# Attention chunks, weight conversion and the offset between two MLP token blocks: moving the second block from seven steps behind the first to four

## Chip, cores and metric

One core of a Trainium2 chip runs the whole kernel. The metric is the device time of one execution in microseconds; the three runs of the kernel before gave 1007.63, 1008.31 and 1009.01, median 1008.31.

## The reference

```python
state = alpha[:, :, t, :, None] * state + np.einsum('bhd,bhe->bhde', k[:, :, t], v[:, :, t])
y[:, :, t] = np.einsum('bhd,bhde->bhe', q[:, :, t], state)
...
h = x @ w_in                       # (3072, 384) @ (384, 2048)
g = h * (1.0 / (1.0 + np.exp(-h)))
x2 = g @ w_out
...
gate = 1.0 / (1.0 + np.exp(-(x2 @ w_gate)))
out = (gate * (x2 @ w_val)) @ w_out2   # d_ff 1536
```

A gated linear attention (4 sequences, 8 heads, 768 tokens, head size 48) feeds an MLP with silu and then a gated MLP, for 3072 tokens of 384 features. Everything is float32 to the user, and the weights arrive as 64-bit floats.

## The kernel before

**Attention.** The tokens are cut into 24 chunks of 128, six to a sequence. For a chunk c, `load_chunk` and `load_values` (L215, L226) fetch its data through SP's queue. `prep` (L262) makes the decays: step 0 is a reversed scan on VectorE (L277), two tiny instructions (L279, L280) and a multiply of k (L285); step 1 a second scan (L287); step 2 a multiply of q (L290). Up to chunk 8 (`ALONE`) the multiplies are GpSimd's, from chunk 9 on VectorE's. `scores` (L297) issues TensorE's transposes of k and the products of k and q; with `apart` the transposes go to a buffer of pool `ps_h`, otherwise to the bank that also takes results. `scores_done` (L318) multiplies by the causal mask on VectorE (L323), copies the transposes on ScalarE (L326) and checks the decays there (L260). `results` (L330) issues the products that give the chunk's output and its addition to the state; `state` (L357) adds that on VectorE (L363, L365) and decays the state (L367, GpSimd up to chunk 8). `y_out` (L377) copies the output on ScalarE and rearranges it with six DMAs (L385, L387). `x_out` (L389) splits it into a rounded part (ScalarE, L394) and a remainder (L396, GpSimd up to chunk 8, then VectorE). The scores of chunk c+1 use the PSUM banks that hold chunk c's addition to the state.

**MLP.** Every product of float32 data is three TensorE products of rounded parts and remainders (`mm3`, L546, L549 to L551). Tokens go in six blocks of 512, so a block is four chunks. One step of the main loop (L754) takes a block b and a slice f of 128 hidden features: `mm_in` (L559) is nine products into h; `act` (L565) is silu (L568), a rounded copy `gh` (L576, ScalarE) and the remainder `gl` (L577, VectorE); `mm_out` (L582) is nine products with `w_out`, issued two steps later through the list `pend`. The list `items` (L725) gives the order: LAG = 7 steps of block 0 alone, then blocks 0 and 1 in turn, then the last LAG slices of block 1, then the other blocks. At a block's end `x2_out` (L595) copies the output from PSUM.

**Weights.** Each slice's 64-bit weights are converted on the way to a slot of rounded part and remainder (class `Way`, L409). The list at L641 has one slot in each of groups 0 to 2 (`in` 0, `in` 1, `out` 0) and two in groups 3 to 16 (`in` g-1 and `out` g-2), one in group 17. A group is made in six bits (`bit`, L507) or two halves (`half`, L526). The first half of group j holds the first two VectorE instructions of group j+1 and one of group j (L459, L494, L461); the second half holds the last two of group j (L496, L497) and the third of group j+1 (L463); ScalarE has L451, L482 and the rounded copy L486, GpSimd the remainder L504. The scratch tiles of a group are reused two groups later.

**Order.** It is written out by hand. In the prefix (L683 to L703), iteration c issues the scores of chunk c+1, the decays of c+2, `x_out` of c-1, the results of c, and then CONV[c] bits. Then each step issues `mm_in`, the chunk work put at (step, place), `act`, `mm_out`, more chunk work, and in the first LAG steps one more half; `act` itself has a half ahead of `gl` (L572) and closes it behind (L578). The tables SCORES and RESULTS (L47, L48) say at which (block, slice, place) a chunk's work stands; `steps` (L706) derives decays and `x_out` from them. Every engine works through its own instructions in the order in which they are issued.

Of the kernel before, what the change touches and what calls it, by code (L numbers as in the profile page):

```python
# [22 lines left out]
NC = NT // C  # L23
# [6 lines left out]
NF1 = FF1 // P  # L30
# [4 lines left out]
NB = len(BLOCKS)  # L35

LEAD = 5
LAG = 7

ALONE = 8  # L40
WARM = 3

BITS = 6
SINGLE = 3
CONV = {1: 5, 2: 5, 3: 6, 4: 5}

SCORES = {6: (0, 1, 0), 7: (0, 3, 0), 8: (0, 5, 0), 9: (1, 10, 0), 10: (1, 11, 1), 11: (1, 13, 0)}  # L47
RESULTS = {5: (0, 0, 0), 6: (0, 2, 0), 7: (0, 4, 0), 8: (0, 6, 0), 9: (1, 11, 0), 10: (1, 12, 1), 11: (1, 14, 0)}  # L48
for _c in range(12, NC):
    SCORES[_c] = (_c // 4 - 1, (0, 4, 8, 11)[_c % 4], 0)  # L50
    RESULTS[_c] = (_c // 4 - 1, (2, 6, 10, 13)[_c % 4], 0)

# [125 lines left out]
def gated_attention_then_mlps(ctx: ExitStack, tc: tile.TileContext, qka, a0, v, w_in, w_out, w_gate, w_val, w_out2, out):  # L178
# [17 lines left out]
    def X(i, dtype=F32):  # L196

        return xp.tile([P, NK, N], dtype, tag=f"x{i}", name=f"x{i}", bufs=1)
# [27 lines left out]
    def load_values(c):  # L226
        vt[c] = ap.tile([P, H, D], F32, tag="v", name="v", bufs=4)
        nc.sync.dma_start(out=vt[c], in_=v[c].rearrange("t (h e) -> t h e", e=D))
# [19 lines left out]
    def warm(n):  # L248

        w = bank(1)[:P]  # L250
        for i in range(n):
            nc.tensor.matmul(w, dg[:, :P], dg[:, :N], start=True, stop=True)
# [41 lines left out]
    def last_of(c):  # L294
        return c % CB == CB - 1
# [343 lines left out]
    with tc.manual_schedule():  # L639
        way1 = Way(  # L640
            [[("in", 0)], [("in", 1)], [("out", 0)]] + [[key for key in (("in", j), ("out", j - 1)) if key[1] < NF1] for j in range(2, NF1 + 1)],  # L641
            lambda j: X(2 * j % 4, U32).rearrange("p k t -> p (k t)"),
            lambda j: X(2 * j % 4 + 1, U32).rearrange("p k t -> p (k t)"),
            lambda n: wp.tile([P, 2, NK, P], F32R, tag="w", name="w"),
        )
        slots2 = [(name, f) for f in range(NF2) for name in ("gate", "val", "out2")]
        NX = 4
        way2 = Way(
            [slots2[n : n + 2] for n in range(0, len(slots2), 2)],
            lambda j: bp["b"].tile([P, 4 * SW], U32, tag="raw", name="raw2", bufs=3),  # L650
            lambda j: bp["b"].tile([P, 4 * SW], U32, tag="tmp", name="tmp2", bufs=3),
            lambda n: (wp if n >= NX else bp["x"]).tile([P, 2, NK, P], F32R, tag="w" if n >= NX else "wx", name="w2"),
        )

        load_chunk(0)
        load_values(0)
        nc.sync.dma_start(out=a0s, in_=a0)
        constants()
        warm(WARM)
        for c in range(1, 4):  # L660
            load_chunk(c)
            load_values(c)
            if c > 1:
                way1.load(c - 2)

        late = []

        def states():
            while late and (last_of(late[0]) or late[0] + 1 in AE):
                c = late.pop(0)  # L670
                if not last_of(c):
                    state(c)

        def results_done(c):
            late.append(c)
            if c >= LEAD:
                states()
            y_out(c)
            if c + 4 < NC:
                load_chunk(c + 4)  # L680
                load_values(c + 4)

        for p0, p1 in ((0, 2), (2, NP)):  # L683
            for s in range(3):
                prep(0, s, p0, p1, nc.vector)
            scores(0, 0, True, p0, p1)
        for s in range(3):
            prep(1, s)
        scores_done(0)
        for c in range(LEAD):  # L690
            scores(c + 1, (c + 1) % 2, True)
            states()
            prep(c + 2, 0)
            scores_done(c + 1)
            prep(c + 2, 1)
            prep(c + 2, 2)
            if c:
                x_out(c - 1)
            results(c, c % 2)
            results_done(c)  # L700
            for _ in range(CONV.get(c, 0)):
                way1.bit()
        states()  # L703
        way1.n_half = 2 * SINGLE

        def steps(items):  # L706

            at = {x: i for i, x in enumerate(items)}
            todo = {}

            def put(i, place, what, c):
                todo.setdefault((i, place), []).append((what, c))

            for c, (b, f, end) in SCORES.items():
                put(at[b, f], end, "scores", c)
                if c > LEAD + 1:
                    put(at[b, f] - 3 if c != ALONE + 1 else at[0, LAG - 2], 2, "prep0", c)
                    put(at[b, f] - 2, 2, "prep1", c)
            for c, (b, f, end) in RESULTS.items():
                put(at[b, f], end, "results", c)  # L720
                put(at[b, f] + 1 if c != ALONE else at[1, NF1 - LAG - 1], 1, "x_out", c)
            put(0, 1, "x_out", LEAD - 1)
            return todo

        items = [(0, f) for f in range(LAG)]  # L725
        for f in range(LAG, NF1):
            items += [(0, f), (1, f - LAG)]
        items += [(1, f) for f in range(NF1 - LAG, NF1)] + [(b, f) for b in range(2, NB) for f in range(NF1)]
        todo = steps(items)

        def tensor(i, place):
            for what, c in todo.get((i, place), ()):
                g = int(c <= ALONE)
                if what == "scores":
                    scores(c, g, False)
                elif what == "results":
                    results(c, g)

        def others(i, place):
            for what, c in todo.get((i, place), ()):  # L740
                if what == "scores":
                    scores_done(c)
                elif what == "results":
                    results_done(c)
                elif what == "x_out":
                    x_out(c)
                elif what == "prep0":
                    prep(c, 0)
                    states()
                elif what == "prep1":  # L750
                    prep(c, 1)
                    prep(c, 2)

        for i, (b, f) in enumerate(items):  # L754
            if (b, f) == (NB - 1, 0):
                at_stack.close()
                bp["b"] = main.enter_context(tc.tile_pool(name="bp", bufs=3))
                bp["x"] = main.enter_context(tc.tile_pool(name="bx", bufs=NX))
                way2.load(0)
                way2.n_half = -2  # L760
            h = mm_in(ps_h, "h", "in", b, f)
            tensor(i, 0)
            way = way1 if i < 2 * NF1 - LAG else way2 if b == NB - 1 else None
            act(b, f, h, None, "out", way)
            others(i, 0)
            others(i, 2)
            if len(pend) > 2:
                mm_out()
            tensor(i, 1)
            others(i, 1)  # L770
            if i < LAG:
                way1.half(True)
                way1.half(False)
            if (b, f) == (NB - 1, NF1 - 4):
                x2_split(0)
            if (b, f) == (NB - 1, NF1 - 1):
                x2_split(1)
        ps_v = None
        items = [(b, f) for f in range(NF2) for b in (0, 1)] + [(b, f) for b in range(2, NB) for f in range(NF2)]
        for b, f in items:  # L780
            if (b, f) == (1, NF2 - 1):
                x2_split(2)
            gate = mm_in(ps_h, "h", "gate", b, f)
            if b == 3 and f % 3 == 0 and f < 9:
                verdict(ps_n, f // 3)
            val = mm_in(ps_v or ps_h, "v" if ps_v else "h", "val", b, f)
            act(b, f, gate, val, "out2", way2 if b < 2 else None)
            if len(pend) > 2:
                mm_out()
            if (b, f) == (2, 1):  # L790
                ps_stack.close()
                ps_v = main.enter_context(tc.tile_pool(name="ps_v", bufs=2, space=PSUM))
                ps_n = main.enter_context(tc.tile_pool(name="ps_n", bufs=1, space=PSUM))
            if f == NF2 - 4 and 1 < b < NB - 1:
                x2_split(b + 1)
        while pend:
            mm_out()
# [46 lines left out]
```

## Time and profile before

| | us |
|---|---|
| median of three runs (lowest, highest) | 1008.31 (1007.63, 1009.01) |
| the profiled execution | 1007.8 |
| its span, first to last instruction | 1006.1 |
| TensorE (PE) busy | 957.5 |
| VectorE (DVE) busy | 521.8 |
| ScalarE (ACT) busy | 385.7 |
| GpSimd (POOL) busy | 127.1 |
| mean granted TensorE clock | 0.975 |

In the rows below, times count from the span's start. A line of a timeline has start, length, engine, line of the kernel, operation, tile written and tiles read, their shapes and the number of instructions merged into it; in brackets is the idle time ahead of it and what ended that. A row of windows has the stretch and its length, then the busy time (with a count) of PE, PEld (weight loads), DVE, ACT and POOL, then the granted clock, the DMA engines' busy share and GB/s. SPq is the queue that issues DMAs.

### The profile page before, as it was taken

The page shows a single profiled execution, that of the slowest core. Times are in us where ns is not written, and L with a number is a line of the kernel's source. Part 1 is how long each engine was busy: PE and PEld are TensorE (multiplying, and loading weights), DVE is VectorE, ACT ScalarE, POOL GpSimd, SP SyncE. Part 2 cuts the span into 40 slices and gives each one's busy share as a digit, 9 for nine tenths or more (in the row PEclk, how much of TensorE's full clock was granted, in tenths as well). Part 3 has the DMA queues.
Part 4 walks back from the last instruction along what each step waited for, and adds up shares of the span by engine and source line. Part 5 has one row for each costly group of instructions (what it writes and reads, how often), then busy time and mean ns, then how long its engine had stood idle before and what let it go on. Part 6 is the DMA issues. An engine that isn't in the chain of part 4 may idle for free.

```text
span 1006.1 us, 12880 instructions
## 1 busy us (share of the span) xinstructions
PE 957.5 (95%) x5008; PEld 786.3 (78%) x5008; DVE 521.8 (52%) x782; ACT 385.7 (38%) x713; POOL 127.1 (13%) x117
## 2 busy tenths in 40 slices
PE   6577899999999999999999999999999999999996
PEld 4465678877888888888888888888888888888885
DVE  8999888464554454453589755663222222222221
ACT  3344566444433433443457443343222222221221
POOL 4554433200000000000033122220000000000000
PEclk8778899999999999999999999999999999999999
DMA  7665352012112112000322111100100000000001
GB/s 184 174 164 160 107 165 83 0 45 87 44 51 80 44 44 78 18 8 13 130 95 94 63 64 64 63 0 1 63 1 1 32 1 0 32 1 1 32 1 35
DMA packets 40038, 58.38 MB, mean 58 GB/s; under 512 B 5216, under 2 KB 28928, under 8 KB 39968
## 3 DMA queue, kind: packets, MB, share of 16 engines
q1 hardware_dynamic: 39968, 57.47, 19.4%
q8 instruction: 41, 0.67, 0.3%
q14 instruction: 29, 0.24, 0.1%
HBM read 48.02 MB, written 4.72 MB: 52 GB/s over the span
## 4 chain that ended last, share of the span: by engine, by line
PE 85%; DVE 9%; issue 2%; POOL 1%; ACT 1%; DMA 1%; SPq 0%; DVEq 0%; POOLq 0%; ACTq 0%
PE h L549 12%; PE h L551 12%; PE h L550 12%; PE s L549 8%; PE s L551 7%; PE s L550 7%; PE y L551 4%; PE y L549 4%; PE y L550 4%; PE v L549 3%; PE v L551 3%; PE v L550 3%; PE s L310 2%; PE y L345 2%; PE y L338 2%
## 5 line engine op out<-in xcount | busy, mean ns | idle before, releaser
L549 PE MATMUL h<-x,w 128*128 128x512 f32 x582 | 228.5, 393 | 4.1 <-ACT w L486 2.3
L551 PE MATMUL h<-x,w 128*128 128x512 f32 x582 | 227.7, 391 | 1.5 <-POOL w L504 1.5
L577 DVE TENSOR_TENSOR gl<-g,gh 128x512 fp32r<-128x512 f32 x168 | 130.0, 774 | 190.8 <-ACT gh L576 190.8
L550 PE MATMUL h<-x,w 128*128 128x512 f32 x582 | 227.5, 391 | 0.0
L576 ACT ACTIVATE gh<-g 128x512 fp32r<-128x512 f32 x168 | 106.2, 632 | 157.9 <-DVE g L571 154.9
L549 PE MATMUL s<-gl,w 128*128 128x512 f32 x336 | 135.8, 404 | 1.5 <-DVE gl L577 1.5
L549 PEld LDWEIGHTS h<-x,w 128*128 128x128 f32 x582 | 109.8, 189 | 29.6 <-ACT w L486 3.5
L550 PE MATMUL s<-gh,w 128*128 128x512 f32 x336 | 132.0, 393 | 0.0
L551 PE MATMUL s<-gh,w 128*128 128x512 f32 x336 | 132.0, 393 | 0.0
L551 PEld LDWEIGHTS h<-x,w 128*128 128x128 f32 x582 | 109.6, 188 | 26.0 <-POOL w L504 2.8
L568 ACT ACTIVATE g<-h 128x512 f32<-128x512 f32 x96 | 57.2, 596 | 184.2 <-PE h L551 184.2
L550 PEld LDWEIGHTS h<-x,w 128*128 128x128 f32 x582 | 109.6, 188 | 23.0
L571 DVE TENSOR_TENSOR g<-v,g 128x512 f32<-128x512 f32 x46 | 31.8, 692 | 178.7 <-PE v L551 178.7
L504 POOL TENSOR_TENSOR w<-tmp,w 128x384 fp32r<-128x384 f32 x36 | 44.3, 1251 | 443.7 <-ACT w L486 443.7
L570 ACT ACTIVATE g<-h 128x512 f32<-128x512 f32 x72 | 43.1, 599 | 144.4 <-PE h L551 144.4
L549 PEld LDWEIGHTS s<-gl,w 128*128 128x128 f32 x336 | 63.5, 189 | 17.5 <-DVE gl L577 1.9
L551 PEld LDWEIGHTS s<-gh,w 128*128 128x128 f32 x336 | 63.7, 189 | 13.8
L550 PEld LDWEIGHTS s<-gh,w 128*128 128x128 f32 x336 | 63.7, 190 | 12.3
L550 PE MATMUL y<-gh,w 128*128 128x512 f32 x168 | 66.0, 393 | 0.0
L549 PE MATMUL y<-gl,w 128*128 128x512 f32 x168 | 65.9, 393 | 0.0
L551 PE MATMUL y<-gh,w 128*128 128x512 f32 x168 | 65.8, 391 | 0.0
L551 PE MATMUL v<-x,w 128*128 128x512 f32 x138 | 53.8, 390 | 0.0
(114 smaller groups left out, 1170.9 us busy)
## 6 DMA issues: line engine op xcount, KB each, us to landing
x<-in_moe_w_out SPq DMA_DIRECT2D x16, 384.0 KB, 4.4
x<-in_qka SPq DMA_DIRECT2D x12, 448.0 KB, 4.3
qk<-in_qka SPq DMA_DIRECT2D x11, 448.0 KB, 4.3
v<-in_v SPq DMA_DIRECT2D x24, 192.0 KB, 4.2
x<-in_moe_w_in SPq DMA_DIRECT2D x16, 288.0 KB, 3.7
raw<-in_moe_w_gate SPq DMA_DIRECT2D x12, 384.0 KB, 3.6
raw<-in_moe_w_val SPq DMA_DIRECT2D x12, 384.0 KB, 3.9
raw<-in_moe_w_out SPq DMA_DIRECT2D x12, 384.0 KB, 3.8
```

The costliest lines, as they stand in the source:

```text
L310: nc.tensor.matmul(S[c][:, j, p * C : (p + 1) * C], t[r : r + D, NP * C + p * C : NP * C + (p + 1) * C], t[r : r + D, p * C : (p + 1) * C] ...
L338: nc.tensor.matmul(y[:DP, p * C : (p + 1) * C], W[:, p], qk[c][:, p * C : (p + 1) * C], start=p == 0, stop=False, skip_group_check=True)
L345: nc.tensor.matmul(y[r : r + D, p * C : (p + 1) * C], vt[c][:, 2 * p + j], m[:, j, p % 2], start=first and p == 0, stop=True, skip_group_c ...
L504: nc.gpsimd.tensor_tensor(l, b[:, i * SW : (i + 1) * SW].bitcast(F32), h.bitcast(F32), op=ALU.subtract)
L549: nc.tensor.matmul(ps, wh, x_l, start=first, stop=False)
L550: nc.tensor.matmul(ps, wh, x_h, start=False, stop=False)
L551: nc.tensor.matmul(ps, wl, x_h, start=False, stop=last)
L568: nc.scalar.activation(g, h, AF.Silu)
L570: nc.scalar.activation(g, h, AF.Sigmoid)
L571: nc.vector.tensor_tensor(g, val, g, op=ALU.mult)
L576: nc.scalar.activation(gh, g, AF.Copy)
L577: nc.vector.tensor_tensor(gl, g, gh.bitcast(F32), op=ALU.subtract)
```

## The change

The second block starts four steps behind the first in place of seven. Chunks 5 to 8 are worked on one to a step in steps 0 to 3 (before: one in two steps, up to step 6). In the prefix 15 bits are converted in place of 21, three in every iteration; step 0 makes six bits in two lots, steps 1 to 3 a first half behind the chunk's state and decays and a second half at the step's end, both behind `gl` rather than around it. From step 4 on `act` takes one half for each step, and steps 6 and 7 get a second one. At the end of block 1, chunks 9 to 12 take one step each in its last four (before: chunks 9 to 11, and chunk 12 in block 2). Slices 14 and 15 of block 0 are issued one after the other. In blocks 0 and 1 the transposes go to `ps_h`. Tables X_OUT and DECAYS place what `steps` had derived.

```diff
-LAG = 7
+LAG = 4
...
-CONV = {1: 5, 2: 5, 3: 6, 4: 5}
-
-SCORES = {6: (0, 1, 0), 7: (0, 3, 0), 8: (0, 5, 0), 9: (1, 10, 0), 10: (1, 11, 1), 11: (1, 13, 0)}
-RESULTS = {5: (0, 0, 0), 6: (0, 2, 0), 7: (0, 4, 0), 8: (0, 6, 0), 9: (1, 11, 0), 10: (1, 12, 1), 11: (1, 14, 0)}
-for _c in range(12, NC):
+CONV = {0: 3, 1: 3, 2: 3, 3: 3, 4: 3}
+
+SCORES = {6: (0, 0, 1), 7: (0, 1, 1), 8: (0, 2, 1), 9: (1, 12, 0), 10: (1, 13, 1), 11: (1, 14, 1), 12: (1, 15, 1)}
+RESULTS = {5: (0, 0, 0), 6: (0, 1, 0), 7: (0, 2, 0), 8: (0, 3, 0), 9: (1, 13, 0), 10: (1, 14, 0), 11: (1, 15, 0), 12: (1, 15, 3)}
+
+X_OUT = {8: (1, 11), 11: (1, 15), 12: (2, 0)}
+
+DECAYS = {7: ((0, 0), (0, 0)), 8: ((0, 1), (0, 1)), 9: ((0, 2), (1, 10)), 10: ((1, 10), (1, 11)), 11: ((1, 12), (1, 13)), 12: ((1, 13), (1, 14))}
+for _c in range(13, NC):
...
-                    put(at[b, f] - 3 if c != ALONE + 1 else at[0, LAG - 2], 2, "prep0", c)
-                    put(at[b, f] - 2, 2, "prep1", c)
+                    first, then = (at[x] for x in DECAYS[c]) if c in DECAYS else (at[b, f] - 3, at[b, f] - 2)
+                    put(first, 2, "prep0", c)
+                    put(then, 2, "prep1", c)
...
-                put(at[b, f] + 1 if c != ALONE else at[1, NF1 - LAG - 1], 1, "x_out", c)
+                put(at[X_OUT[c]] if c in X_OUT else at[b, f] + 1, 1, "x_out", c)
...
-        for f in range(LAG, NF1):
+        for f in range(LAG, NF1 - 2):
             items += [(0, f), (1, f - LAG)]
+        items += [(0, NF1 - 2), (0, NF1 - 1), (1, NF1 - LAG - 2), (1, NF1 - LAG - 1)]
...
-                    scores(c, g, False)
+                    scores(c, g, items[i][0] < 2)
...
+        def convert(i):
+            if i == 0:
+                for _ in range(BITS // 2):
+                    way1.bit()
+            else:
+                way1.half(True)
+                way1.half(False)
...
-            way = way1 if i < 2 * NF1 - LAG else way2 if b == NB - 1 else None
+            way = way1 if LAG <= i < 2 * NF1 - LAG else way2 if b == NB - 1 else None
             act(b, f, h, None, "out", way)
             others(i, 0)
             others(i, 2)
+            if i < LAG:
+                convert(i)
             if len(pend) > 2:
                 mm_out()
-            tensor(i, 1)
-            others(i, 1)
-            if i < LAG:
-                way1.half(True)
-                way1.half(False)
+            for place in (1, 3):
+                tensor(i, place)
+                others(i, place)
+            if i < LAG or LAG + 2 <= i < LAG + 4:
+                convert(i)
```

## Rows read from the trace of the kernel before

**Rows 1.** Page: the span.
```profile
span 1006.1 us, 12880 instructions
```

**Rows 2.** Windows: prefix, steps 0 to 6, after (stretch, length, busy by engine, clock).
```profile
20.40:59.19 38.79, 23.93 (x232) 21.39 (x232) 36.72 (x52) 15.55 (x41) 22.33 (x22) 0.74 0.60 163
...
59.19:122.86 63.67, 50.09 (x305) 38.16 (x305) 57.27 (x73) 31.34 (x63) 28.04 (x24) 0.84 0.52 143
...
122.86:250.00 127.14, 122.60 (x656) 100.37 (x657) 81.80 (x124) 65.54 (x122) 25.43 (x21) 1.00 0.26 75
```

**Rows 3.** Waits of PE from 122.86 to 250 us: total, times, longest.
```profile
PE s L310 <- ACT x L600: 2.0, 1, 2.0
...
PE s L549 <- DVE gl L577: 1.5, 1, 1.5
```

**Rows 4.** Timeline, PE: step 8's first product and the tenth.
```profile
127.80 0.39 PE L549 MATMUL h<-x,w 128*128 128x512 f32 x1
...
129.84 0.39 PE L549 MATMUL s<-gl,w 128*128 128x512 f32 x1
```

**Rows 5.** Windows: a pair's halves; state; mask and first scan; second scan.
```profile
140.25:142.06 1.81, 1.81 (x9) 1.50 (x9) 1.81 (x3) 1.78 (x3) 0.00 (x0) 1.00 0.53 151
...
142.67:145.00 2.33, 2.33 (x12) 1.94 (x11) 2.29 (x5) 0.76 (x2) 0.15 (x1) 1.00 0.55 169
...
225.81:226.57 0.76, 0.76 (x4) 0.62 (x5) 0.71 (x3) 0.24 (x1) 0.00 (x0) 1.00 0.00 0
...
230.09:232.85 2.76, 2.76 (x14) 2.28 (x13) 2.69 (x6) 1.09 (x4) 0.00 (x0) 1.00 0.62 189
...
235.37:236.59 1.22, 1.22 (x6) 0.98 (x7) 1.22 (x2) 0.59 (x1) 0.00 (x0) 1.00 0.00 0
```

**Rows 6.** DVE by line, steps 0 to 6: busy, mean ns, idle before, releaser.
```profile
L463 DVE SCALAR_TENSOR_TENSOR x<-x 128x768 f32<-128x768 f32 x7 | 12.9, 1847 | 0.1
...
L459 DVE TENSOR_SCALAR x<-x 128x768 uint32<-128x768 uint32 x7 | 5.7, 808 | 5.6 <-POOL w L504 5.6
```

**Rows 7.** Timeline, DVE and POOL, end of step 1's conversion.
```profile
81.38 3.68 DVE L463 SCALAR_TENSOR_TENSOR x<-x 128x768 f32<-128x768 f32 x1
...
82.27 1.97 POOL L504 TENSOR_TENSOR w<-x,w 128x384 fp32r<-128x384 f32 x2
```

**Rows 8.** Timeline, DVE: first and fourth of the bits that leave.
```profile
47.07 2.10 DVE L459 TENSOR_SCALAR x<-x 128x384 uint32<-128x384 uint32 x1
...
50.46 0.36 DVE L494 TENSOR_SCALAR x<-x 128x384 uint16<-128x384 uint16 x1
```

**Rows 9.** Timeline: rounded copy, product, silu, copy of g.
```profile
81.49 0.94 ACT L486 ACTIVATE w<-x 128x384 fp32r<-128x384 f32 x2 [4.31 <-DVE x L497]
...
82.06 0.50 PE L549 MATMUL h<-x,w 128*128 128x512 f32 x1 [0.82 <-ACT w L486]
...
82.33 0.58 ACT L568 ACTIVATE g<-h 128x512 f32<-128x512 f32 x1
...
82.94 0.63 ACT L576 ACTIVATE gh<-g 128x512 fp32r<-128x512 f32 x1
```

**Rows 10.** Timeline, PE: small products behind three different waits.
```profile
64.65 2.05 PE L338 MATMUL y<-qk,state 112*112 112x128 f32 x8 [3.12 <-POOL state L367]
...
97.04 1.13 PE L338 MATMUL y<-x,state 112*112 112x128 f32 x8
...
77.41 1.20 PE L345 MATMUL y<-m,v 128*48 128x128 f32 x16 [1.69 <-ACT x L394]
```

**Rows 11.** Timeline, SP: four of a chunk's six result copies.
```profile
127.79 2.49 SPq L387 DMA_DIRECT2D xf<-xs  x4
```

**Rows 12.** Timeline: chunk 11's result, its x_out, block 2's first product.
```profile
235.37 0.60 ACT L382 ACTIVATE xs<-y 112x512 f32<-112x512 f32 x1 [0.63 <-PE y L345]
...
240.94 0.53 ACT L394 ACTIVATE x<-xf 128x384 fp32r<-128x384 f32 x1
...
242.31 0.47 PE L549 MATMUL h<-x,w 128*128 128x512 f32 x1 [0.60 <-DVE x L396]
```

## The prediction, made before the changed kernel was run

> **What bounds the kernel now.** I read the page first for the span, then the busy time of the engines over three stretches, then who keeps TensorE waiting, then VectorE's instructions by line, and last the timeline around single waits. "Step i" is the i-th pass of the main loop, T0 to T7 the start on TensorE of the first product of that step (59.19 us for T0, 122.86 us for T7), and a "group" is one entry of the conversion list (groups 0 to 2 hold one weight slot, 3 to 17 hold two). The profiled execution took 1007.8 us with a span of 1006.1 [rows 1]; the median of the three runs is 0.5 us above it.
>
> From T7 to 250 us TensorE is busy 122.60 of 127.14 us [rows 2], and the longest of its few waits are one of 2.0 and one of 1.5 us [rows 3]. Nine large products take 2.04 us there [rows 4], so a step (nine in, nine out) is 4.1 us of pure TensorE time. Ahead of T7 it is VectorE that is full: 36.72 of 38.79 us in the later prefix, 57.27 of 63.67 us in steps 0 to 6, with TensorE at a mean granted clock of 0.74 and 0.84 [rows 2]. So the time is, in essence, the moment at which VectorE lets TensorE run freely, plus the TensorE work then left.
>
> VectorE's 63.67 us hold more than work. Undisturbed, a pair of slots costs it 1.81 us in its first half and 2.33 us in its second, 4.1 us together; a chunk costs 0.76 (state), 2.76 (mask, first scan and what hangs on it) and 1.22 us (second scan), 4.7 together [rows 5]. In steps 0 to 6 one of the pair's six instructions alone averages 1847 ns, and the first of a pair stands idle 5.6 us in all behind GpSimd's subtraction of an earlier pair [rows 6]. Why: an instruction of VectorE on SBUF that starts while GpSimd works doesn't advance until GpSimd is done. The 3.68 us of the one at 81.38 end at 85.06, a little after GpSimd's 1.97 us ending at 84.24; undisturbed it ends within the 2.33 us of its half [rows 5, 7].
>
> The Trainium skill ("SBUF — State Buffer", section "SBUF: two separate sides") states this as a rule: one shared pair of ports, held for the whole instruction, the loser fully blocked. By that rule, with all of GpSimd's time added to VectorE's, the sum below would stand some 13 us higher. The trace agrees for this instruction but not for the stretch: 28.04 us of GpSimd fit beside 57.27 of VectorE in 63.67 us [rows 2].
>
> **The parts of the change.**
>
> *Prefix.* Six bits of conversion leave it (21 to 15). Four of them stood ahead of T0: the first starts at 47.07 us, the fourth at 50.46 and takes 0.36, so 3.75 us pass [rows 8]. The new bits of iteration 0 fill VectorE time that is nearly all busy already [rows 2], so nothing more is won: T0 moves from 59.2 to about 55.6. Bounds: 0 (if GpSimd's x_out ends last anyway) to 5.
>
> *Work put off.* At T7 now, seven products in and five out are done. By the new order the like point, TensorE free, with chunks up to 8 done, is T4: four in and two out. Six times 2.04 us, **+12.2 us**, come afterwards [rows 4]. Against that VectorE has three pairs fewer to make by then.
>
> *Steps 0 to 3.* This is the large term. Before, step i makes the pair that step i+2 multiplies; VectorE works a step behind TensorE and hardly ever waits for it. After, step i makes what step i+1 multiplies (group 3 in step 1, and `in` slot 2 is wanted in step 2). Then the two wait in turn. The chain, from before's rows: with the second half's last add done, ScalarE's rounded copy starts at 81.49 and the first product at 82.06 [rows 9]; the products then wait about 1 us for GpSimd's remainder (1.97 us for two slots [rows 7]), so 3.1 us in place of 2.04 until h is whole; silu 0.58 and the copy 0.63 us [rows 9]; only then `gl`, which now stands first in VectorE's order, and the state update behind it, which wants the chunk's results from TensorE. All the rest of the step's VectorE work, the conversion included, is queued behind these.
> The price depends on TensorE's clock. Behind a wait of 3.12 us eight small products took 2.05 us; without one the same eight took 1.13 [rows 10]. These are the two levels, 1.2 and 2.4 GHz. In the new steps 2 and 3 TensorE stands idle 4 us and more ahead of each step, so I take the lower level: h 4.3 us, results 3.7 (2.05 for the first eight, the rest partly recovered).
> Laid out by hand: step 0: VectorE's work 9.8 us (a state, a gl of 0.7, two scans, the second half of group 2, a mask, the first half of group 3, what is left of group 2's first half), 1.8 waiting for the first h, 2.6 behind GpSimd: 14.2, to 69.8. Step 1: gl 0.7, chunk 4.7, pair to its add 3.3, GpSimd 3.5: 12.2, to 82.0. Step 2: 0.6 to the first product, h and results 8.0, then state 0.8, first scan with its multiplies on VectorE 2.4, half a pair 1.8, mask 1.2, the two adds 1.5, GpSimd 1.7: 17.9, to 99.9. Step 3, without a scan or mask: 0.6, 8.0, 0.8, 1.8, 1.5, GpSimd 2.0: 14.7, to 114.6. T4 is 0.6 behind, **115.2**.
> The unknown is GpSimd: I charged 9.8 us of its roughly 22 in these steps (28.04 less three pairs at 1.97 [rows 2, 7]). In steps 0 to 6 VectorE lost about a third of GpSimd's time (nearest row, 28.04 us [rows 2]); that would be 7.3. I take the middle, 8.5: T4 is 113.9. Bounds: 7 and 22 of GpSimd; clock high or low, some 4.4.
>
> *After T4.* The first products run at the lower level: +2.0. Steps 4 to 7 make three pairs in 16.4 us of TensorE; with about 6 us for each (4.1 and a third of the 5.6 behind GpSimd [rows 5, 6]) and four gl VectorE needs 21, but a step's second products come two steps later, so TensorE has that much to go on: of the waits, today's 1.5 us [rows 3] falls away and about 0.5 comes, -1.0.
>
> *Chunks 9 to 12.* They move to the last four steps of block 1; chunk 12, moved ahead of block 2, is the same TensorE work earlier, cost 0. VectorE needs about 7.5 us for each (4.7, a gl, and the multiplies that GpSimd does for earlier chunks), in steps of 4.1 plus 3.7 for the chunk's products: covered. SP issues for each chunk six result copies (four of them 2.49 us [rows 11]) and its loads, some 5 us, under the step, here and in steps 0 to 3. The seam costs: chunk 11's ScalarE copy began at 235.37 and its x_out at 240.94, 5.6 us later, and block 2 waited 0.60 [rows 12], with a whole step between. Now only one mm_out (2.04), scores and results of chunk 12 lie between, and x_out is queued on ScalarE behind that chunk's checks: TensorE waits about 0.7 for the mask and 1.6 for x_out, 1.7 more than today; the 2.0 us wait at block 0's end [rows 3] loses some 0.3. **+1.4**; bounds 0 and 4. Transposes into an `h` buffer free TensorE of waits where it isn't the bound: 0.
>
> *Sum.* T4 113.9 + 12.2 - 122.9 = +3.2; + 2.0 - 1.0 + 1.4 = **+5.6**: 1013.4 for the profiled execution's 1007.8, **1013.5** as a median between this and its 0.5 more.
>
> **Rivals.**
> *VectorE stays fed (faster).* If gl and the state of steps 2 and 3 find their inputs ready, these steps cost VectorE's own work: about 11 and 8 us in place of 17.9 and 14.7. That takes 13.6 off: T4 100, and 1000 in all. For it: now VectorE idles only 6.4 us in steps 0 to 6, 5.6 of them behind GpSimd [rows 2, 6], and that idling should vanish as the chunk's work stands between the pairs. It decides at gl of steps 2 and 3: below 2 us of idle there it wins; half of it is 1006. Chance 0.30.
> *The clock holds (same).* If TensorE stays at the upper level, h and results take 2.2 us less in each of two steps and the 2.0 after T4 goes: -6.4, about 1007 to 1009. For it: 16 products behind a wait of 1.69 us took 1.20, no longer than at the upper level [rows 10]. Against: the 3.12 us above. Chance 0.13.
> *Steps 4 to 10 starve (slower still).* If `in` slots 5 and 6 come late, VectorE's 21 us against 16.4 show up as TensorE waits: up to +4.4, 1017. Chance 0.15, inside the slower cases.
> *The seam alone.* T4 comes out even and only block 2's start is late: 1010. Chance 0.10, slower too.
>
> **How the numbers follow.** The forecast has 0.32; with its two neighbours slower has 0.57, the seam and the starved steps included. A measurement of this kernel tells about 0.2% (2 us) from no change. The range goes from most of the fed case (1001) to the starved one with a full charge for GpSimd (1019), and leaves out the fully fed case and full blocking. The slower cases' own range is 1010 to 1019.
>
> **What would show it.** Right: first product of step 0 near 55.6; VectorE idle 3 us or more ahead of gl in steps 2 and 3; TensorE idle over 4 us ahead of steps 3 and 4, with a clock of 0.5 behind; T4 after 110; no idle of VectorE behind GpSimd's subtraction at a pair's start; block 2's first product waiting about 2 us. Wrong: T4 below 108 (the break-even, 122.9 less 12.2 less the 2.4 that follow), or gl in steps 2 and 3 without a wait.

## The result and the profile after

The change made the kernel slower: 1016.54 us median of four runs (1015.94 to 1018.67) against 1008.64 of the kernel before on the same chip, a ratio of 1.0084 with a 95% interval of 1.0066 to 1.0101. The forecast was 1013.5 within 1001 to 1019. The profiled execution took 1015.96 us with a span of 1014.2, against 1007.8 and 1006.1 [rows 1]. The changed file has four more lines ahead of the functions, so L463 in it is L459 of before, L501 is L497, L553 is L549, L581 is L577.

The windows of the changed kernel, cut at its own T0 and T4, answer to [rows 2]:

```profile
20.40:56.23 35.83, 25.15 (x233) 22.14 (x232) 30.29 (x50) 14.19 (x38) 24.16 (x22) 0.67 0.54 150
56.23:113.54 57.31, 34.33 (x251) 26.92 (x251) 40.18 (x59) 24.00 (x51) 21.57 (x19) 0.75 0.47 129
113.54:250.00 136.46, 133.31 (x716) 108.60 (x716) 93.32 (x140) 73.46 (x134) 29.77 (x26) 0.98 0.29 84
```

In steps 0 to 3 VectorE is busy 40.18 of 57.31 us (70%), where it had 57.27 of 63.67 (90%). Nothing is full in this stretch any more: TensorE 60%, GpSimd 38%, at a mean granted TensorE clock of 0.75. What VectorE waited for is in its waits from 56.23 to 135 us (total, times, longest):

```profile
DVE gl L581 <- ACT gh L580: 13.9, 3, 5.6
DVE x L463 <- DMA x<-in_moe_w_out: 8.9, 2, 6.2
DVE state L367 <- PE s L359: 2.2, 2, 1.2
```

And TensorE, from 55 to 330 us, answering to [rows 3]:

```profile
PE h L553 <- ACT w L490: 17.9, 3, 8.5
...
PE s L553 <- ACT x L604: 2.9, 1, 2.9
...
PE s L314 <- ACT x L604: 1.4, 1, 1.4
PE h L553 <- DVE x L400: 1.4, 1, 1.4
...
PE y L349 <- issue: 0.8, 1, 0.8
```

The first rows of the two lists belong together: TensorE waited three times, 17.9 us, for ScalarE's rounded weights (L490), which wait for VectorE's last add; VectorE waited three times, 13.9 us, for `gl`'s input, which waits for TensorE. The timeline of steps 2 to 4 shows one turn after the other:

```profile
81.47 0.96 DVE L501 TENSOR_TENSOR x<-x 128x768 f32<-128x768 f32 x1
...
82.46 0.94 ACT L490 ACTIVATE w<-x 128x384 fp32r<-128x384 f32 x2 [3.52 <-DVE x L501]
83.03 0.80 PE L553 MATMUL h<-x,w 128*128 128x512 f32 x1 [8.46 <-ACT w L490]
...
87.60 0.60 ACT L572 ACTIVATE g<-h 128x512 f32<-128x512 f32 x1 [4.21 <-PE h L555]
...
88.89 0.69 DVE L581 TENSOR_TENSOR gl<-g,gh 128x512 fp32r<-128x512 f32 x1 [5.60 <-ACT gh L580]
...
99.49 0.80 PE L553 MATMUL h<-x,w 128*128 128x512 f32 x1 [5.28 <-ACT w L490]
...
105.35 0.69 DVE L581 TENSOR_TENSOR gl<-g,gh 128x512 fp32r<-128x512 f32 x1 [5.60 <-ACT gh L580]
...
113.54 0.80 PE L553 MATMUL h<-x,w 128*128 128x512 f32 x1 [4.13 <-ACT w L490]
...
120.03 0.56 DVE L463 TENSOR_SCALAR x<-x 128x768 uint32<-128x768 uint32 x1 [6.23 <-DMA x<-in_moe_w_out]
```

The first product of each of these steps takes 0.80 us in place of the 0.50 in [rows 9]: the lower clock (granted 0.50 over the nine products of steps 2 and 3 and the first twelve from step 4 on), after waits of 8.46, 5.28 and 4.13 us. From the first product of step 2 to silu 4.57 us pass. The last line is a wait that the prediction did not have.

The starts of steps, read from the first product of each in the timeline of TensorE, serve as milestones for all runs. By step 12 every version has done the same TensorE work (12 slices in, 10 out, chunks up to 8); by step 35, in block 2, the seam is behind it too.

| profiled execution | step 0 | 2 | 4 | 5 | 12 | 35 | span |
|---|---|---|---|---|---|---|---|
| before | 59.2 | 73.4 | 94.9 | 103.4 | 146.0 | 258.1 | 1006.1 |
| after | 56.2 | 83.0 | 113.5 | 120.7 | 150.4 | 266.5 | 1014.2 |

So of 8.1 us in the span, 4.4 are lost ahead of step 12 and 4.0 between step 12 and step 35; behind that the two run alike within 0.3 us.

### The profile page after: what moved, and what is told of

It reads as the page before. It is cut to its first block, busy times and chain, and to the rows that moved or that the text cites. A ratio compares the mean times of both kernels' runs of the same rounds, so it can differ in the third digit from the quotient of the medians.

```text
span 1014.2 us, 12894 instructions
## 1 busy us (share of the span) xinstructions
PE 959.3 (95%) x5008; PEld 788.2 (78%) x5008; DVE 510.4 (50%) x782; ACT 386.2 (38%) x713; POOL 126.2 (12%) x117
## 3 DMA queue, kind: packets, MB, share of 16 engines
q1 hardware_dynamic: 39968, 57.47, 19.3%
## 4 chain that ended last, share of the span: by engine, by line
PE 87%; DVE 4%; DMA 2%; POOL 2%; issue 1%; ACT 1%; SPq 1%; DVEq 0%; ACTq 0%; POOLq 0%
PE h L553 13%; PE h L555 13%; PE h L554 13%; PE s L553 8%; PE s L554 7%; PE s L555 7%; PE y L555 4%; PE y L554 4%; PE y L553 4%; PE v L553 3%; PE v L554 3%; PE v L555 3%; PE y L349 2%; PE y L342 2%; PE s L314 2%
## 5 line engine op out<-in xcount | busy, mean ns | idle before, releaser
L553 PE MATMUL h<-x,w 128*128 128x512 f32 x582 | 230.1, 395 | 20.4 <-ACT w L490 17.9
L581 DVE TENSOR_TENSOR gl<-g,gh 128x512 fp32r<-128x512 f32 x168 | 130.8, 779 | 197.2 <-ACT gh L580 197.2
L553 PEld LDWEIGHTS h<-x,w 128*128 128x128 f32 x582 | 110.4, 190 | 44.8 <-ACT w L490 18.9
L553 PE MATMUL s<-gl,w 128*128 128x512 f32 x336 | 134.7, 401 | 3.0 <-ACT x L604 2.9
L508 POOL TENSOR_TENSOR w<-tmp,w 128x384 fp32r<-128x384 f32 x36 | 44.3, 1251 | 431.9 <-ACT w L490 431.9
L553 PEld LDWEIGHTS s<-gl,w 128*128 128x128 f32 x336 | 63.3, 188 | 18.9 <-ACT x L604 3.3
L553 PE MATMUL y<-gl,w 128*128 128x512 f32 x168 | 65.5, 390 | 0.0
```

The costliest lines, as they stand in the source:

```text
L508: nc.gpsimd.tensor_tensor(l, b[:, i * SW : (i + 1) * SW].bitcast(F32), h.bitcast(F32), op=ALU.subtract)
L553: nc.tensor.matmul(ps, wh, x_l, start=first, stop=False)
L581: nc.vector.tensor_tensor(gl, g, gh.bitcast(F32), op=ALU.subtract)
```

## Experiments

Seven variants and the changed kernel itself ran, four on one chip (e1 to e4) and four on another (e5 to e8), each with the kernel before beside it. Its median was 1009.18 us on the first and 1009.68 on the second chip. The same milestones for all:

| profiled execution | step 0 | 2 | 4 | 5 | 12 | 35 | span | median of runs (range) |
|---|---|---|---|---|---|---|---|---|
| e1_seam | 55.9 | 82.3 | 111.6 | 118.0 | 147.8 | 260.8 | 1007.8 | 1013.59 (1009.48 to 1016.80) |
| e2_early | 58.2 | 80.0 | 101.9 | 106.5 | 145.8 | 265.0 | 1012.2 | 1012.74 (1010.30 to 1013.93) |
| e3_ahead | 56.2 | 86.7 | 112.2 | 117.2 | 147.1 | 265.3 | 1012.4 | 1016.22 (1014.11 to 1016.42) |
| e4_fill | 56.3 | 83.9 | 111.5 | 118.0 | 149.4 | 265.9 | 1013.2 | 1015.08 (1014.58 to 1015.50) |
| e5_early_load | 58.3 | 80.0 | 101.9 | 106.5 | 141.4 | 257.5 | 1004.8 | 1008.02 (1006.53 to 1009.52) |
| e6_all | 58.6 | 80.3 | 102.8 | 107.4 | 142.2 | 255.3 | 1002.7 | 1004.47 (1003.96 to 1005.18) |
| e7_load | 56.3 | 85.6 | 115.9 | 122.9 | 152.6 | 269.0 | 1016.7 | 1018.28 (1016.29 to 1019.05) |
| e8_same | 56.6 | 86.1 | 116.5 | 123.6 | 153.3 | 269.5 | 1017.6 | 1018.44 (1018.30 to 1019.39) |

**The lead given back.** e2_early:

```diff
-CONV = {0: 3, 1: 3, 2: 3, 3: 3, 4: 3}
+CONV = {0: 4, 1: 4, 2: 4, 3: 4, 4: 5}
...
-            if i == 0:
-                for _ in range(BITS // 2):
-                    way1.bit()
-            else:
-                way1.half(True)
-                way1.half(False)
+            way1.half(True)
+            way1.half(False)
```

> Prefix with 21 bits again (4, 4, 4, 4, 5) and halves from step 0 on, so step i makes the pair of step i+2 as before; the offset of four steps, a chunk in each step and the tail stay. Theory (the lost step of lead makes TensorE and VectorE wait in turn): step 0 starts 3 to 4 us later (59 to 60), VectorE's idle ahead of gl in steps 2 and 3 (5.6 us each) goes below 2 us, step 4 starts near 97 to 103, the time is 1003 to 1009. Rival (VectorE and GpSimd are simply full with a chunk to a step): one more pair ahead of step 4 costs 4 to 7 us, step 4 starts at 117 or later and the time is 1019 to 1024.

The theory holds for steps 0 to 5, though VectorE makes one pair more by then: step 0 starts 1.9 us later (3 to 4 expected), step 4 starts at 101.9 in place of 113.5, step 5 at 106.5 in place of 120.7, and VectorE's three waits for `gl` from 58 to 135 us come to 3.8 us in place of 13.9. The rival asked for 117 or later. The time missed the expected range all the same (ratio to before 1.0029, 1.0017 to 1.0040), because of what came next:

```profile
102.89 1.16 SPq L389 DMA_DIRECT2D xf<-xs  x2
...
104.09 2.49 SPq L391 DMA_DIRECT2D xf<-xs  x4
...
106.68 0.52 SPq L227 DMA_DIRECT2D qk<-in_qka  x1
...
108.24 0.38 SPq L436 DMA_DIRECT2D x<-in_moe_w_in  x1
...
116.39 0.56 DVE L463 TENSOR_SCALAR x<-x 128x768 uint32<-128x768 uint32 x1 [6.30 <-DMA x<-in_moe_w_out]
...
118.94 0.80 PE L553 MATMUL s<-gl,w 128*128 128x512 f32 x1 [5.88 <-DVE gl L581]
```

These are lines of the timeline of e2_early in the order of time: SP issues the chunk's six result copies, then the next chunk's loads, and only then the weights. VectorE stands 6.30 us for them, and TensorE 5.88 us for the `gl` queued behind that instruction.

**The loads ahead of the chunk's copies.** e5_early_load is e2_early and

```diff
+        def ahead(self):
+            j = self.n_half // 2
+            if self.early != j:
+                self.early = j
+                self.b_scalar(j, 0)
+                self.load(j + 2)
...
                 else:
-                    self.b_scalar(j, 0)
-                    self.load(j + 2)
+                    self.ahead()
                     self.a_scalar(j + 1)
...
+            if 0 <= i < LAG:
+                way1.ahead()
             others(i, 0)
```

> As the run with 21 early bits, and in steps 0 to 3 ScalarE's first copy of a pair and the weight loads behind it are issued ahead of the chunk's result copies and loads. Theory: in that run step 5 began 14 us earlier than in the changed kernel, and most was given back in one place, where VectorE stood 6.3 us for weights whose loads SP issued behind the chunk's six copies and three loads, and TensorE 5.9 us for gl behind it. Then that wait falls below 1 us, step 12 begins at 138 to 141 in place of 145.8, and the time is 1003 to 1008. Rival (the loads land late because the transfers themselves are slow, or ScalarE's copy delays the chunk as much): step 12 stays at 145 or later, 1011 to 1014.

Step 5 is at the same 106.5, and VectorE has no wait for a weight load left from there on; step 12 moves from 145.8 to 141.4. That is 0.4 short of the expected milestone (TensorE still has three waits for `gl` of 1.3 to 1.5 us on the way), but the time, 1008.02, is where the theory had it. The ratio to before is 0.9986 (0.9976 to 0.9996).

e7_load has the same edit (from step 1 on) on the changed kernel, without the lead.

> The changed kernel with only the loads of steps 1 to 3 issued ahead of the chunk's copies, without the lead. Theory: VectorE's 6.2 us wait for weights in step 4 goes, but TensorE had waited only 0.4 us behind it, since it ran at the lower clock: less than 2 us gained, 1014 to 1017. Rival (the late loads are the whole of the loss): 1008 to 1011.

Measured 1018.28, above the expected range, but beside 1018.44 for the changed kernel itself on this chip (e8_same). The long wait for weights (5.4 us in e8_same) is gone from its list of VectorE's waits and nothing is won: VectorE waits longer for `gl` instead (19.3 us in place of 16.3 from 55 to 135 us), and from step 4 to step 12 it takes 36.7 us in place of 36.8. My reading, which no run tests alone: without the lead TensorE runs at the lower clock behind T4 (granted 0.50) and does not need that pair sooner. The same late load costs nothing in one version and 4.7 us (1012.74 to 1008.02, on two chips) in another.

e7_load and e5_early_load ran on one chip, and apart from step 0's loads only the lead is between them: 1018.28 and 1008.02, so with the loads early the lead is worth 10.3 us of the whole time.

> The changed kernel again, unchanged, beside the other runs on one chip: 1015 to 1018; if it comes out below 1013, differences of 2 us between runs on different chips carry nothing.

It came out at 1018.44, ratio 1.0082 (1.0065 to 1.0099): the ratio repeats, the absolute time is 0.4 above the expected 1018.

**The seam.** e1_seam:

```diff
-... 12: ((1, 13), (1, 14))}
+... 12: ((1, 13), (1, 14)), 13: ((2, 2), (2, 2))}
```

> Only the decays of chunk 13 move, from slices 1 and 2 of block 2 to slice 2, so that VectorE's copy of block 1's output no longer stands behind a scan, a multiply and a state update. If the 2.9 us wait of the first mm_out of block 2 is that copy's place in VectorE's order: the wait falls below 0.5 us and the time by 2 to 3 us against the changed kernel (1013.5 to 1014.5). If ScalarE's copies or the PSUM banks themselves set it, the wait and the time stay (1016 to 1017). Nothing ahead of 245 us moves under either.

In the changed kernel TensorE's first product of block 2's `mm_out` waits 2.86 us for ScalarE's copy of a bank (L604), which follows VectorE's copy (L606); that stands in VectorE's order behind a scan, two multiplies and a state update of chunks 12 and 13. The state update of chunk 12 is issued with chunk 13's decays, so the edit moves it too. In the kernel before, the same copy (L602) stood behind chunk 13's scan and multiply as well, but not behind the state update, and TensorE worked on chunk 12's results (L345, L355) meanwhile:

```profile
254.43 1.08 PE L345 MATMUL y<-m,v 128*48 128x128 f32 x16
254.57 0.68 DVE L602 COPY x<-s 128x512 f32<-128x512 f32 x1
...
255.29 0.60 ACT L600 ACTIVATE x<-s 128x512 f32<-128x512 f32 x1 [2.14 <-DVE x L602]
255.34 0.53 PE L355 MATMUL s<-v,kt 128*48 128x48 f32 x16
...
255.94 0.50 PE L549 MATMUL s<-gl,w 128*128 128x512 f32 x1
```

Then the changed kernel's timeline:

```profile
259.36 1.22 DVE L281 TENSOR_TENSOR_SCAN G<-qk,dg 112x511 f32<-112x511 f32 x1
...
259.54 0.60 ACT L604 ACTIVATE x<-y 128x512 f32<-128x512 f32 x1 [0.84 <-PE y L555]
...
262.97 0.69 DVE L606 COPY x<-s 128x512 f32<-128x512 f32 x1
263.70 0.60 ACT L604 ACTIVATE x<-s 128x512 f32<-128x512 f32 x1 [3.56 <-DVE x L606]
...
264.35 0.50 PE L553 MATMUL s<-gl,w 128*128 128x512 f32 x1 [2.86 <-ACT x L604]
```

and that of e1_seam:

```profile
256.82 0.68 DVE L606 COPY x<-s 128x512 f32<-128x512 f32 x1
257.02 0.60 ACT L604 ACTIVATE x<-y 128x512 f32<-128x512 f32 x1 [0.84 <-PE y L555]
257.54 0.60 ACT L604 ACTIVATE x<-s 128x512 f32<-128x512 f32 x1
...
258.80 0.39 PE L553 MATMUL s<-gl,w 128*128 128x512 f32 x1
```

The wait is gone, and from step 12 to step 35 it takes 113.0 us in place of 116.1 (before: 112.1). Its median lies in the expected range, but its runs scatter over 7 us, so that median alone, ratio 1.0059 (1.0038 to 1.0079), would not have shown it; and its profile is 2.6 us early at step 12 already, ahead of anything that the edit moves. The same edit on top of e5_early_load is e6_all:

> As the run before in this list, with the decays of chunk 13 moved to slice 2 of block 2. If the three causes (lost lead, late loads, the copy at block 1's end) are separate and add up: 2 to 3 us below that run, 1001 to 1005, below both kernels. If they cover each other: like that run.

1004.47 against 1008.02 on one chip, with ranges that don't meet, and 113.0 us from step 12 to 35 against 116.1: 3.1 us, so the seam adds to the other two causes. Those two don't simply add: the late loads cost nothing without the lead (e7_load). Against the kernel before the ratio is 0.9945 (0.9931 to 0.9960). This version beats both kernels, with the offset of four steps and a chunk in each.

**The half ahead of gl.** e3_ahead puts the first half back around `gl` in steps 1 to 3:

```diff
-            way = way1 if LAG <= i < 2 * NF1 - LAG else way2 if b == NB - 1 else None
+            way = way1 if 1 <= i < 2 * NF1 - LAG else way2 if b == NB - 1 else None
...
-            if i < LAG:
+            if i < 1:
                 convert(i)
             if len(pend) > 2:
```

> In steps 1 to 3 the first half of a pair stands around gl, as before the change, in place of behind the chunk's work; all else is the changed kernel. Theory (waits in turn): the half's 1.9 us fall into the 5.6 us in which VectorE idles for gl in steps 2 and 3, so steps 3 and 4 start 1.9 and 3.8 us earlier, and the pair loads are issued ahead of the chunk's copies, so the 6.2 us wait for a load in step 4 shrinks: 1011 to 1013. Rival (VectorE's and GpSimd's throughput sets these steps): the order changes nothing, 1015 to 1018.

The expected gain is there where it was expected: step 2 to 3 takes 14.7 us in place of 16.5, step 3 to 4 10.9 in place of 14.0, and `gl` waits 1.85 and 1.45 us in place of 5.60. Yet step 2 starts 3.7 us later than in the changed kernel's profile. A part of that is the edit: in step 1 the half ahead of `gl` waits for its weights, and the state update and the scores queue behind it.

```profile
56.24 0.80 PE L553 MATMUL h<-x,w 128*128 128x512 f32 x1 [0.78 <-POOL x L400]
...
75.06 0.56 DVE L463 TENSOR_SCALAR x<-x 128x768 uint32<-128x768 uint32 x1 [2.09 <-DMA x<-in_moe_w_out]
...
78.34 2.08 PE L314 MATMUL s<-x 48*128 48x128 f32 x16 [6.56 <-DVE G L277]
```

Another part is not: the first line shows step 0 at the lower clock, and e8_same, the unedited kernel, starts step 2 at 86.1 behind the same 0.80 us. Against that execution step 2 is 0.6 us later, step 4 4.2 and step 12 6.1 us earlier; at the seam 1.9 us go again, where block 2's first nine products run at a granted clock of 0.53. But the profiled run is the fastest of e3_ahead by 2 us, and the runs, with a ratio of 1.0075 (1.0058 to 1.0092), don't tell it from the changed kernel; the expected time was missed, and what the order gains in the end stays open. Order alone, in any case, doesn't repair a missing lead.

**The clock.** e4_fill adds `warm(n)`, dummy products whose result nothing reads:

```diff
+FILL = {1: 6, 2: 4, 3: 3}
...
             for place in (1, 3):
                 tensor(i, place)
                 others(i, place)
+            if i in FILL:
+                warm(FILL[i])
```

> Adds 6, 4 and 3 dummy products to TensorE's idle time at the ends of steps 1, 2 and 3 (their result is not used); nothing else changes. If the lower clock is part of the price: h of steps 2 and 3 takes about 3.1 in place of 4.3 us, step 4 starts 3 to 4 us earlier, the products behind it run at the upper level; of the 2.8 us that this gives back, about 2 are lost again to the pair whose weights land late, so 1011 to 1013. If the clock doesn't matter because VectorE is full anyway: 1015 to 1018, with step 4 still at 113.

Between the first products of steps 2 and 3 pass 14.3 us in place of 16.5: h of step 2 runs at the upper level. In steps 3 and 4 it falls to the lower one after the first products (granted 0.72 and 0.78 over h). From step 2 to step 4 it takes 27.6 us in place of 30.5; step 4 starts 2.0 us earlier, less than expected, and about half of this is lost again, where VectorE waits for the late weights and TensorE behind it:

```profile
119.23 0.56 DVE L464 TENSOR_SCALAR x<-x 128x768 uint32<-128x768 uint32 x1 [7.48 <-DMA x<-in_moe_w_out]
...
123.80 0.50 PE L554 MATMUL h<-x,w 128*128 128x512 f32 x1 [1.54 <-ACT w L491]
```

Step 12 is 1.0 us earlier, and the time 1015.08 with a ratio of 1.0063 (1.0046 to 1.0080). The clock is a part of the price, some 1 to 3 us here, not its cause; the run tells little more, as it lies at the edge of both expectations and the dummies don't hold the clock throughout.

## Why the prediction was right

The direction, the range and the main mechanism held; the forecast was 3 us low, and nearly all of that sits in one term.

*Prefix.* T0 was put at 55.6 and came at 56.23, again on GpSimd's `x_out`: 3.0 us won in place of 3.6.

*Steps 0 to 3.* T4 was put at 113.9 and came at 113.54. So close an agreement is luck in part: e8_same, the same code, has its T4 at 116.45. The details named beforehand are there: `gl` waits 5.60 us in steps 2 and 3 (3 or more predicted), TensorE stands idle 5.28 and 4.13 us ahead of steps 3 and 4 (over 4), the clock behind these is the lower level, T4 lies above 110, and no wait for GpSimd's subtraction stands at the start of a pair in steps 1 to 3. e2_early shows that this is the lost lead: with the pair made one step sooner the waits go and step 5 comes 14 us earlier. The rival "VectorE stays fed" fell at the place named for it, `gl` of steps 2 and 3.

*GpSimd.* I charged 8.5 us, between a third and all of its time. Set against the usual length of the same form, VectorE's instructions in steps 0 to 3 are by my estimate 7.1 us longer (the two second scans, L291, take 2.15 and 2.18 us in place of 1.22), beside GpSimd's 21.57: a third, less than charged. The third had been read off the kernel before, though, and there the same comparison gives 13.4 us beside 28.04, nearly half. So that the charge came out near is luck too. The third instruction of a pair, 1847 ns in [rows 6], averages this in steps 0 to 3:

```profile
L467 DVE SCALAR_TENSOR_TENSOR x<-x 128x768 f32<-128x768 f32 (+1 forms) x5 | 4.4, 887 | 0.7 <-ACT x L455 0.6
```

One of the five is the single slot's, and still the price has halved: in the changed order the remainder of a pair (L508) mostly runs while VectorE waits for `gl`, so the rule of full blocking from the Trainium skill ("SBUF — State Buffer", "SBUF: two separate sides") finds little to block. All of GpSimd's time, as the prediction took the rule, would have been some 14 us too much here.

*Work put off.* T4 plus the 12.2 us, less the old T7 of 122.86, is +2.9 (+3.2 predicted).

*After T4.* The lower clock lasts until 119.14: 12 products take 5.6 us where they take 2.7 at the upper level, +2.9 (+2.0 predicted). TensorE's waits behind that point, for `gl` and for GpSimd's remainders, fell from 1.9 us (1.5 of them [rows 3]) to 0.4, -1.5 (-1.0 predicted). What the prediction missed is VectorE's wait for weights, 6.23 us at 120.03. I had added up SP's issues for a chunk (some 5 us) and found that they fit under a step, but not looked at what is queued behind them: the pair's weight loads. In the changed kernel the miss costs nothing, as e7_load shows; in e2_early it is the largest loss.

*The seam.* This is the term that was mis-sized: +1.4 predicted, with bounds of 0 and 4; +3.9 measured. TensorE waits 1.41 (block 0's copy), 0.84 (the wait that the view puts down to "issue"; by its place, the mask of chunk 12), 1.40 (`x_out` of chunk 11) and 2.86 us, 6.5 in all, against 2.04 and 0.60 before [rows 3, 12]. The first three are as predicted. The last is the step that failed: "chunk 12, moved ahead of block 2, is the same TensorE work earlier, cost 0". Its results had stood on TensorE between the second slice of block 2 and the first `mm_out`, and had covered the copy of block 1's output; with them gone, and chunk 12's state update ahead of it, the copy's place in VectorE's order is bare.

By these terms +2.9 + 2.9 - 1.5 + 3.9 = +8.2, against 8.1 in the spans.

*The other rivals.* The clock did not hold (0.80 us for the first products of steps 2, 3 and 4), steps 4 to 10 did not starve (0.4 us of waits), and the seam is half of the loss, not all of it.

## What to carry to other kernels

When work is made just ahead of its use, count by how many steps it leads. Here, with a lead of two steps the maker and the user each run through, with one they wait in turn, and the busy share falls (VectorE from 90% to 70%) while the time grows. To move work is to take it away from where it stood: look at what it covered there, and on every queue, DMA issue included, at what now stands behind it. A wait can be hidden by another loss, so a fix that gains nothing alone may be worth several microseconds once the other is mended.

## What was not expected of the hardware

The first product of step 0 comes behind a wait of 1.08 us in the changed kernel's profile and runs at the upper level (0.50 us, granted clock 1.00); in e8_same, the same code, it comes behind 0.77 us and runs at the lower one (0.80, granted 0.50). VectorE's first `gl` then waits 4.54 us in place of 2.67, and step 2 starts at 86.1 in place of 83.0. Ahead of step 4, in reverse, 4.13 us of waiting led to the lower level and 4.12 us in e1_seam to the upper at first (0.50). So the length of the wait alone does not tell TensorE's clock, and with it 3 us differ between executions of one code. That may be why e1_seam scatters by 7 us where the kernel before, beside it, scatters by 2.4: over its four runs, from 1009.48 to 1016.80 us, the mean granted clock falls from 0.967 to 0.966, 0.963 and 0.961. It is not shown, as there is a trace of the fastest one alone.

```profile
56.65 0.80 PE L553 MATMUL h<-x,w 128*128 128x512 f32 x1 [0.77 <-POOL x L400]
...
62.18 0.69 DVE L581 TENSOR_TENSOR gl<-g,gh 128x512 fp32r<-128x512 f32 x1 [4.54 <-ACT gh L580]
...
86.10 0.80 PE L553 MATMUL h<-x,w 128*128 128x512 f32 x1 [9.25 <-ACT w L490]
```

These three lines are of e8_same's timeline.
